# A gated GLU behind an FFT filter: x and the filter loaded as plain fp32 on one ordered SP queue, casts on GpSimd, and a main loop issued in the order it is written

## The chip, the core and the metric

The kernel runs on one NeuronCore of one Trainium2 chip. The metric is the device time of one execution in microseconds; before the change the median of 3 runs is 386.45 us (383.33 to 387.43).

## The reference

For `x` of shape (8, 3200, 256) in fp32, each channel is filtered along the sequence by a spectrum, and a causal gated linear unit follows:

```python
X = np.fft.rfft(x, axis=1)
y = np.fft.irfft(X * (filt_r + 1j * filt_i)[None], n=3200, axis=1)
gate_pre[s] = sum_k conv_w[k] * y_padded[s + k]          # 5 taps, causal
out = (sigmoid(gate_pre) * (y @ w_val)) @ w_out
```

## The kernel before

The transform of length 3200 is done as 128 x 25: a 128-point stage, a pass through a scratch in DRAM that reorders, and a 25-point stage; then the same backwards. Each batch goes through seven stages, and each stage cuts a batch into seven chunks, so that there are 56 chunks in all:

- `load_x` brings a chunk of `x` into a bf16 tile `xt` (4 or 3 rows of 256 for each of 128 partitions). It is issued on the GpSimd queue, whose DMA casts fp32 to bf16 on the way (line 86).
- `s1` multiplies `xt` by the constant `cf_t` (line 307), VectorE evicts PSUM into `so` (line 310), and SP writes `so` to the scratch `dscr` (line 312).
- `load_t` reads `dscr` back in another order into `tt` (lines 326 to 329). Each chunk of `tt` holds rows of all seven `dscr` writes of its batch.
- `s2` multiplies `tt` by `wc_t`, `ws_t`, `wsn_t` (lines 340 to 346). ScalarE evicts into `xs` (line 349). VectorE multiplies by the filter with two products `za`, `zb` and their sum `z` (lines 354, 358, 360). All three have two bf16 inputs in SBUF.
- `inva` is the inverse of that stage (lines 376, 378); ScalarE evicts into `u` (line 381), SP writes `escr` (line 392) and `load_v` reads it back into `vt` (line 398).
- `invb` is the inverse 128-point stage (line 413); ScalarE evicts into `yt` (line 415). For the first chunk of a batch GpSimd fills the four rows ahead of the sequence (a memset on line 420, two copies on line 422).
- `conv` (line 431, sigmoid on ScalarE on line 436), `val` (line 448, the product `gv` on VectorE on line 453) and `outp` (line 465) end the chunk; `o` is evicted by VectorE for even chunks (line 470) and by ScalarE for odd ones (line 473), and SP stores it (line 475).

Every matmul stage takes one tile `ps` from a PSUM pool of four tiles of 128 x 1024 fp32. A stage therefore may start only when the tile taken four stages earlier has been evicted.

A loop over G writes one chunk of each stage per step, with lags: `s1` works on chunk G, `s2` on G-9, `inva` on G-10, `invb` on G-19, `conv` on G-21, `val` on G-22, `outp` on G-23. Within a step the order is invb, s2, conv, s1, inva, val, outp. A scheduler then orders each engine's instructions by priority and by its own estimate of when they are ready; TensorE's and ScalarE's stand as written, but on VectorE `so` stands ahead of `z` in three of the seven steps of a batch. The seven `load_t` of a batch are issued together, and so are the seven `load_v`.

Ahead of the loop VectorE and ScalarE compute the transform matrices from iotas (`cf_t`, `wc_t` and so on). `floormod` (lines 103 to 113) takes seven VectorE instructions for each of six arguments; `expand` (line 171) makes a matrix with 13 instructions; `dg_t` (line 284) takes 20; `fm_t` (lines 232, 234) two large ones. The filter comes in 24 DMAs on the GpSimd queue, cast to bf16.

Of the kernel before, what the change touches and what calls it, by code (L numbers as in the profile page):

```python
# [15 lines left out]
PI = math.pi  # L16
# [19 lines left out]
def kernel(  # L36
# [31 lines left out]
    b_npi = cpool.tile([128, 1], FP32, name="b_npi")  # L68
# [3 lines left out]
    xpool = ctx.enter_context(tc.tile_pool(name="xin", bufs=10))  # L72
    spool = ctx.enter_context(tc.tile_pool(name="s1o", bufs=4))
    tpool = ctx.enter_context(tc.tile_pool(name="s2i", bufs=8))

    def psum():
        return pp.tile([128, 1024], FP32, name="ps", tag="ps")

# [3 lines left out]
    def load_x(b, j):  # L82
        p0, np_ = PCH[j]
        xt = xpool.tile([128, 4, D], BF16, name="xt")
        src = x[b].rearrange("(a r) d -> a r d", r=R)[:, p0:p0 + np_, :]
        nc.gpsimd.dma_start(out=xt[:, 0:np_, :], in_=src)  # L86
        xts[(b, j)] = xt

    for j in range(NCH):
        load_x(0, j)  # L90


    with tc.tile_pool(name="gen", bufs=1) as g1, \
         tc.tile_pool(name="gen2", bufs=2) as g2, \
         tc.tile_pool(name="genf", bufs=1) as gf:

        def floormod(src_ap, divisor):
            shp = list(src_ap.shape)
            divi = g2.tile(shp, I32, name=f"fm_i{shp[1]}")
            bak = g2.tile(shp, FP32, name=f"fm_b{shp[1]}")  # L100
            q = g2.tile(shp, FP32, name=f"fm_q{shp[1]}")
            cm = g2.tile(shp, FP32, name=f"fm_c{shp[1]}")
            nc.vector.tensor_scalar(divi[...], src_ap, 1.0 / float(divisor), None,
                                    op0=ALU.mult)
            nc.vector.tensor_copy(bak[...], divi[...])
            nc.vector.scalar_tensor_tensor(q[...], bak[...], -float(divisor), src_ap,
                                           op0=ALU.mult, op1=ALU.add)
            nc.vector.tensor_scalar(cm[...], q[...], float(divisor) - 0.5, None,
                                    op0=ALU.is_ge)
            nc.vector.scalar_tensor_tensor(q[...], cm[...], -float(divisor), q[...],  # L110
                                           op0=ALU.mult, op1=ALU.add)
            nc.vector.tensor_scalar(cm[...], q[...], -0.5, None, op0=ALU.is_lt)
            nc.vector.scalar_tensor_tensor(q[...], cm[...], float(divisor), q[...],
                                           op0=ALU.mult, op1=ALU.add)
            return q

        def iota(shape, pattern, base, cm, name):
            t = g1.tile(shape, FP32, name=name)
            nc.gpsimd.iota(t[...], pattern=pattern, base=base, channel_multiplier=cm,
                           allow_small_or_imprecise_dtypes=True)  # L120
            return t

        nc.vector.memset(b_npi[:, :], -PI)
        pcol = iota([128, 1], [[0, 1]], 0, 1, "pcol")


        kc = iota([128, NG, 2, GL], [[5, NG], [0, 2], [1, GL]], 1, 0, "kc")
        nc.vector.memset(kc[:, NG - 1, 0, GL - 1:GL], 0.0)
        pr = g1.tile([128, NG, 2, GL], FP32, name="pr")
        nc.vector.tensor_scalar(pr[...], kc[...], pcol[:, 0:1], None, op0=ALU.mult)  # L130
        nc.vector.tensor_scalar(pr[:, :, 0, :], pr[:, :, 0, :], 0.75 * L, None,
                                op0=ALU.add)
        q = floormod(pr[...].rearrange("p g c l -> p (g c l)"), L)
        nc.scalar.activation(cf_t[:, :], q[...], AF.Sin, bias=b_npi[:, 0:1],
                             scale=2.0 * PI / L)

        ident = g1.tile([128, 128], FP32, name="ident")
        nc.vector.memset(ident[:, :], 1.0)
        nc.gpsimd.affine_select(out=ident[:, :], in_=ident[:, :], pattern=[[1, 128]],
                                compare_op=ALU.is_equal, fill=0.0, base=0,  # L140
                                channel_multiplier=-1)
        idh = g1.tile([128, 128], FP16, name="idh")
        nc.vector.tensor_copy(idh[:, :], ident[:, :])


        rq = floormod(pcol[...], R)
        lp = g1.tile([128, 1], FP32, name="lp")
        nc.vector.tensor_tensor(lp[...], pcol[...], rq[...], op=ALU.subtract)
        nc.vector.tensor_scalar(lp[...], lp[...], 1.0 / R, None, op0=ALU.mult)
        rp = g1.tile([128, 1], FP32, name="rp")  # L150
        nc.vector.tensor_copy(rp[...], rq[...])
        lw = g1.tile([128, 1], FP32, name="lw")
        nc.vector.tensor_scalar(lw[...], pcol[...], 4.0 * R - 0.5, None, op0=ALU.is_ge)
        nc.vector.tensor_scalar(lw[...], lw[...], -65.0, None, op0=ALU.mult)


        mk = g1.tile([128, GL, R], FP16, name="mk")
        mkf = g1.tile([128, GL, R], FP32, name="mkf")
        nc.vector.memset(mkf[...], 1.0)
        nc.gpsimd.affine_select(out=mkf[...], in_=mkf[...], pattern=[[-R, GL], [0, R]],  # L160
                                compare_op=ALU.is_ge, fill=0.0, base=0,
                                channel_multiplier=1)
        nc.gpsimd.affine_select(out=mkf[...], in_=mkf[...], pattern=[[R, GL], [0, R]],
                                compare_op=ALU.is_ge, fill=0.0, base=R - 1,
                                channel_multiplier=-1)
        nc.vector.tensor_copy(mk[...], mkf[...])

        def expand(dst, src):
            nc.gpsimd.memset(dst[:, :, P2:128], 0.0)
            for g in range(NG):  # L170
                nc.vector.tensor_tensor(
                    dst[:, g, 0:P2].rearrange("p (l r) -> p l r", l=GL),
                    src[:, g, :].unsqueeze(1).to_broadcast((128, GL, R)),
                    mk[...], op=ALU.mult)

        def negate(dst, src):
            nc.vector.tensor_scalar(dst[...], src[...], -1.0, None, op0=ALU.mult)

        def sincos(prod, dc, ds, dsn):
            qs = floormod(prod[...].rearrange("p g r -> p (g r)"), N)  # L180
            sn = g2.tile([128, NG, R], FP16, name="sn")
            nc.scalar.activation(sn[...].rearrange("p g r -> p (g r)"), qs[...],
                                 AF.Sin, bias=b_npi[:, 0:1], scale=2.0 * PI / N)
            pc = g2.tile([128, NG, R], FP32, name="pc")
            nc.vector.tensor_scalar(pc[...], prod[...], 0.75 * N, None, op0=ALU.add)
            qc = floormod(pc[...].rearrange("p g r -> p (g r)"), N)
            cs = g2.tile([128, NG, R], FP16, name="cs")
            nc.scalar.activation(cs[...].rearrange("p g r -> p (g r)"), qc[...],
                                 AF.Sin, bias=b_npi[:, 0:1], scale=2.0 * PI / N)
            expand(dc, cs)  # L190
            expand(dsn, sn)
            negate(ds, dsn)

        HK = R // 2 + 1
        kv = g1.tile([128, NG, R], FP32, name="kv")
        nc.gpsimd.iota(kv[:, :, 0:HK], pattern=[[5, NG], [L, HK]], base=1,
                       channel_multiplier=0, allow_small_or_imprecise_dtypes=True)
        nc.gpsimd.iota(kv[:, :, HK:R], pattern=[[5, NG], [-L, R - HK]],
                       base=1 + L * (R - 1), channel_multiplier=0,
                       allow_small_or_imprecise_dtypes=True)  # L200
        nc.vector.tensor_scalar(kv[...], kv[...], lp[:, 0:1], None, op0=ALU.add)
        nc.vector.tensor_scalar(kv[:, NG - 1, :], kv[:, NG - 1, :], lw[:, 0:1], None,
                                op0=ALU.add)
        nc.vector.tensor_scalar(kv[...], kv[...], rp[:, 0:1], None, op0=ALU.mult)
        sincos(kv, wc_t, ws_t, wsn_t)


        fi_t = gf.tile([128, NG, D], BF16, name="fi_t")

        def fsrc(f, row, ap):  # L210
            return bass.AP(tensor=f.tensor, offset=f.offset + row * D, ap=ap + [[1, D]])

        for f, dst in ((filt_r, fr_t), (filt_i, fi_t)):
            for l in range(GL):
                ng = NG if l < GL - 1 else NG - 1
# [187 lines left out]
    def invb(b, j):  # L403
# [15 lines left out]
        if j == 0:  # L419
            nc.gpsimd.memset(y[:, :, 0:H, 0:1], 0.0)  # L420
            for dh in range(2):
                nc.gpsimd.tensor_copy(y[:, dh, 0:H, 1:L], y[:, dh, R:R + H, 0:L - 1])
# [68 lines left out]
    for G in range(total):  # L491
        c = at(G, -NCH)
        if c is not None:
            load_x(*c)
# [57 lines left out]
```

## Time and profile before

| | |
|---|---|
| median of 3 runs | 386.45 us |
| the profiled execution's own time | 387.95 us |
| its span, first to last instruction | 385.9 us |
| mean granted TensorE clock | 0.966 |
| busy: TensorE / VectorE / ScalarE / GpSimd | 312.3 / 284.9 / 229.1 / 64.2 us |
| first `s2` matmul | 45.09 us |
| first `invb` matmul | 92.66 us |
| GpSimd DMA issues of `xt` | 56, 30.2 us in all |
| GpSimd copies on line 422 | 16, 9.3 us in all |

The span is 2.05 us shorter than the profiled execution's time; that part lies outside the first and last instruction. Busy time of TensorE comes from modelled ends of pipelined matmuls, so a full digit in its row doesn't say that it runs at its peak. Idle time of an engine is put down to what released it last.

### The profile page before, as it was taken

The numbers are of one execution on the slowest core, as the hardware profiler recorded it, in microseconds if no ns is written. First come the engines' busy times: TensorE is split into PE (matmuls) and PEld (weight loads), VectorE is DVE, ScalarE is ACT, GpSimd is POOL, SyncE is SP. The second block draws the span as 40 slices with busy tenths as digits, with TensorE's granted clock in tenths as the row PEclk, the third lists the DMA queues.
The fourth block names the chain that finished last, engine by engine and source line by source line (L and its number), as shares of the span: only waits on it lengthen the run. The fifth ranks groups of instructions, "written<-read, shape, count | busy, mean of one in ns | idle before, by whom it ended". The sixth has DMA issues, their size and how long they took to land.

```text
span 385.9 us, 8019 instructions
## 1 busy us (share of the span) xinstructions
PE 312.3 (81%) x3089; PEld 206.9 (54%) x3089; DVE 284.9 (74%) x462; ACT 229.1 (59%) x255; POOL 64.2 (17%) x131
## 2 busy tenths in 40 slices
PE   0230477475899999999997999899999999999992
PEld 0100145253656756766675666566676677666661
DVE  4999958553858887888787789678977677765554
ACT  1100235334976777677765776677677878867660
POOL 8797211112110211021102011100010001001000
PEclk9999998766989999999999999999999999999998
DMA  7999999999999999999999999989595968449343
GB/s 124 144 162 190 216 257 251 231 250 280 179 250 249 311 286 273 263 282 332 274 301 303 286 269 298 285 299 319 201 351 170 304 223 299 136 142 323 141 191 152
DMA packets 94118, 94.53 MB, mean 245 GB/s; under 512 B 10102, under 2 KB 74624, under 8 KB 94080
## 3 DMA queue, kind: packets, MB, share of 16 engines
q1 hardware_dynamic: 80064, 78.98, 62.5%
q0 software_dynamic: 14016, 15.04, 28.1%
q8 instruction: 24, 0.39, 0.4%
q14 instruction: 14, 0.11, 0.1%
HBM read 56.59 MB, written 52.43 MB: 282 GB/s over the span
## 4 chain that ended last, share of the span: by engine, by line
PE 44%; DVE 20%; DMA 19%; SPq 8%; issue 4%; ACT 2%; POOL 1%; DVEq 0%; ACTq 0%; POOLq 0%
PE ps L431 12%; PE ps L448 7%; DMA escr<-u 6%; PE ps L465 6%; DVE so L310 6%; DMA vt<-escr 5%; SPq L326 5%; PE ps L413 5%; DMA dscr<-so 4%; PE ps L376 3%; DVE gv L453 3%; DMA tt<-dscr 3%; PE ps L378 3%; PE ps L307 3%; DVE za L354 2%
## 5 line engine op out<-in xcount | busy, mean ns | idle before, releaser
L415 ACT ACTIVATE yt<-ps 128x1024 bf16<-128x1024 f32 (+1 forms) x56 | 52.1, 931 | 44.3 <-PE ps L413 44.2
L453 DVE TENSOR_TENSOR gv<-ps,gt 128x1024 bf16<-128x1024 f32 (+1 forms) x56 | 61.9, 1104 | 18.7 <-PE ps L448 13.7
L310 DVE CAST so<-ps 128x1024 bf16<-128x1024 f32 (+1 forms) x56 | 61.5, 1103 | 19.0 <-PE ps L307 15.9
L354 DVE TENSOR_TENSOR za<-xs,fr_t 125x1024 bf16<-125x1024 bf16 (+1 forms) x56 | 37.3, 665 | 50.5 <-ACT xs L349 50.3
L381 ACT ACTIVATE u<-ps 125x1024 bf16<-125x1024 f32 (+1 forms) x56 | 53.9, 963 | 24.4 <-PE ps L378 21.6
L431 PE MATMUL ps<-yt,dg_t 64*64 64x512 bf16 (+1 forms) x1120 | 65.7, 361 | 0.8
L349 ACT ACTIVATE xs<-ps 125x1024 bf16<-125x1024 f32 (+1 forms) x56 | 54.0, 965 | 19.6 <-PE ps L346 18.4
L436 ACT ACTIVATE gt<-ps 128x1024 bf16<-128x1024 f32 (+1 forms) x56 | 52.4, 935 | 9.1 <-PE ps L431 5.9
L86 POOL DMA_DIRECT2D xt<-in_x_dram x56 | 30.2, 569 | 153.0 <-PE ps L307 146.5
L307 PE MATMUL ps<-xt,cf_t 128*128 128x512 bf16 x112 | 36.9, 421 | 22.4 <-DVE so L310 11.4
L465 PE MATMUL ps<-wo_t,gv 128*128 128x256 bf16 x400 | 52.8, 273 | 0.9 <-DVE gv L453 0.9
L448 PE MATMUL ps<-yt,wv_t 128*128 128x512 bf16 (+1 forms) x224 | 52.6, 357 | 0.0
L465 PEld LDWEIGHTS <-gv 128*128 128x128 bf16 x400 | 39.1, 98 | 14.9 <-DVE gv L453 1.2
L413 PE MATMUL ps<-ci_t,vt 128*128 128x128 f16 x400 | 31.9, 221 | 13.3 <-DMA vt<-escr 9.6
L431 PEld LDWEIGHTS <-dg_t 64*64 64x64 bf16 x1120 | 30.1, 106 | 23.2 <-issue 10.1
L340 PE MATMUL ps<-tt,wc_t 125*128 125x256 bf16 x104 | 30.1, 289 | 12.9 <-DMA tt<-dscr 10.6
L470 DVE COPY o<-ps 128x1024 f32<-128x1024 f32 (+1 forms) x32 | 36.7, 1148 | 1.1 <-PE ps L465 1.1
L360 DVE TENSOR_TENSOR z<-za,zb 125x1024 bf16<-125x1024 bf16 (+1 forms) x56 | 36.4, 650 | 1.3
L413 PEld LDWEIGHTS <-vt 128*128 128x128 bf16 x400 | 27.0, 98 | 17.9 <-DMA vt<-escr 10.7
L358 DVE TENSOR_TENSOR zb<-xs,fm_t 125x1024 bf16<-125x1024 bf16 (+1 forms) x56 | 36.2, 646 | 0.0
L376 PE MATMUL ps<-z,vc_t 125*128 125x256 bf16 x104 | 30.0, 289 | 6.9 <-DVE z L360 6.9
L307 PEld LDWEIGHTS <-cf_t 128*128 128x128 f16 x112 | 9.2, 108 | 41.7 <-issue 28.2
(109 smaller groups left out, 386.6 us busy)
## 6 DMA issues: line engine op xcount, KB each, us to landing
out_dram<-o SPq DMA_DIRECT2D x32, 512.0 KB
tt<-dscr SPq DMA_DIRECT2D x48, 256.0 KB
escr<-u SPq DMA_DIRECT2D x48, 224.0 KB
out_dram<-o SPq DMA_DIRECT2D x24, 384.0 KB
xt<-in_x_dram POOLq DMA_DIRECT2D x32, 256.0 KB, 6.5
dscr<-so SPq DMA_DIRECT2D x32, 256.0 KB
vt<-escr SPq DMA_DIRECT2D x32, 256.0 KB
xt<-in_x_dram POOLq DMA_DIRECT2D x24, 192.0 KB, 5.7
```

The source lines that it names most:

```text
L307: nc.tensor.matmul(ps[:, a * D:e * D], lhsT=cf_t[:, 0:128], rhs=xt[:, a:e, :], start=True, stop=True)
L310: nc.vector.tensor_copy(so[:, 0:np_, :].rearrange("p a d -> p (a d)"), ps[:, 0:np_ * D])
L349: nc.scalar.activation(xs[0:P2, 0:ng, :, :].rearrange("p g c d -> p (g c d)"), ps[0:P2, 0:ng * 512], AF.Copy)
L354: nc.vector.tensor_tensor(za[0:P2, 0:ng], xs[0:P2, 0:ng], fr_t[0:P2, g0:g0 + ng, :].unsqueeze(2).to_broadcast((P2, ng, 2, D)), op=ALU.mult)
L381: nc.scalar.activation(u[0:P2, 0:2 * ng, :].rearrange("p q d -> p (q d)"), ps[0:P2, 0:ng * 512], AF.Copy)
L413: nc.tensor.matmul(ps[:, o:o + L], lhsT=v[:, a, 128 * dh:128 * dh + 128], rhs=ci_t[:, :], start=True, stop=True)
L415: nc.scalar.activation(y[:, :, H + p0:H + p0 + np_, :].rearrange("p h a n -> p h (a n)"), ps[:, :].rearrange("p (h n) -> p h n", h=2)[:, : ...
L431: nc.tensor.matmul(ps[64 * dh:64 * dh + 64, 512 * r:512 * r + np_ * L], lhsT=dg_t[rows, dh, k, :], rhs=y[rows, dh, p0 + k:p0 + k + np_, :] ...
L436: nc.scalar.activation(g[:, :, 0:np_ * L], ps[:, :].rearrange("p (h n) -> p h n", h=2)[:, :, 0:np_ * L], AF.Sigmoid)
L448: nc.tensor.matmul(ps[:, 512 * eh:512 * eh + np_ * L], lhsT=wv_t[:, dh, 128 * eh:128 * eh + 128], rhs=y[:, dh, H + p0:H + p0 + np_, :], st ...
L453: nc.vector.tensor_tensor(gv[:, :, 0:np_ * L], ps[:, :].rearrange("p (h n) -> p h n", h=2)[:, :, 0:np_ * L], g[:, :, 0:np_ * L], op=ALU.mult)
L465: nc.tensor.matmul(ps[:, D * a:D * a + D], lhsT=gv[:, eh, L * a:L * a + L], rhs=wo_t[:, eh, :], start=(eh == 0), stop=(eh == 1))
```

## The change

- `load_x` is issued on SP, without a cast, into fp32 tiles `xf` (six buffers). A new stage `cast_x` on GpSimd copies `xf` into the bf16 `xt`, which has four buffers where it had ten.
- The filter is loaded as fp32 into `ff` by the same 24 transfers, on SP. VectorE casts the real part to `fr_t`, ScalarE makes `fm_t` from the imaginary part.
- `s1` of the first batch stands ahead of the computation of the other matrices; three of its seven evictions go to ScalarE. `load_t` of the first batch alternates with `load_x` of the second.
- The matrices are computed with three VectorE instructions in `sine` in place of seven in `floormod`, with one instruction per `expand` in place of 13, and with the negation and `dg_t` on ScalarE.
- The rows ahead of the sequence are filled by VectorE, in one memset and one copy.
- SP is issued in written order throughout, and in the main loop TensorE, ScalarE and VectorE too. Lags grow: `s2` 10, `inva` 11, `invb` 21, `conv` 23, `val` 24, `outp` 25. `load_t` and `load_v` are issued one chunk per step. `za` and `zb` have two buffers, `o` three.

```diff
@@ loads
-        xt = xpool.tile([128, 4, D], BF16, name="xt")
-        src = x[b].rearrange("(a r) d -> a r d", r=R)[:, p0:p0 + np_, :]
-        nc.gpsimd.dma_start(out=xt[:, 0:np_, :], in_=src)
-        xts[(b, j)] = xt
+        xf = fpool.tile([128, 4, D], FP32, name="xf")
+        src = x[b].rearrange("(a r) d -> a r d", r=R)[:, p0:p0 + np_, :]
+        nc.sync.dma_start(out=xf[:, 0:np_, :], in_=src)
+        xts[(b, j)] = xf
+
+    def cast_x(b, j):
+        np_ = PCH[j][1]
+        xf = xts[(b, j)]
+        xt = xpool.tile([128, 4, D], BF16, name="xt")
+        nc.gpsimd.tensor_copy(xt[:, 0:np_, :], xf[:, 0:np_, :])
+        xts[(b, j)] = xt
@@ s1
-        nc.vector.tensor_copy(so[:, 0:np_, :].rearrange("p a d -> p (a d)"),
-                              ps[:, 0:np_ * D])
+        if b == 0 and j % 2 == 1:
+            st[("Sact", j)] = nc.scalar.activation(sov, ps[:, 0:np_ * D], AF.Copy)
+        else:
+            nc.vector.tensor_copy(sov, ps[:, 0:np_ * D])
@@ ahead of the loop
+        for j in range(NCH):
+            s1(0, j)
+            if 1 <= j <= GL:
+                load_f(j - 1)
...
+        for j in range(NCH):
+            load_t(0, j)
+            load_x(1, j)
@@ invb
-            nc.gpsimd.memset(y[:, :, 0:H, 0:1], 0.0)
-            for dh in range(2):
-                nc.gpsimd.tensor_copy(y[:, dh, 0:H, 1:L], y[:, dh, R:R + H, 0:L - 1])
+            nc.vector.memset(y[:, :, 0:H, 0:1], 0.0)
+            nc.vector.tensor_copy(y[:, :, 0:H, 1:L], y[:, :, R:R + H, 0:L - 1])
@@ main loop
+    steps = [
+        (invb, LAG_IB, 0), (s2, LAG_S2, 0), (conv, LAG_IB + 2, 0), (cast_x, -2, 1),
+        (s1, 0, 1), (inva, LAG_S2 + 1, 0), (load_x, -NCH, 2), (load_t, NCH, 1),
+        (load_v, LAG_S2 + 1 + NCH, 0), (val, LAG_IB + 3, 0), (outp, LAG_IB + 4, 0),
+    ]
+    with tc.manual_schedule(engines={E.SP, E.PE, E.Activation, E.DVE}):
+        for G in range(total):
+            for stage, lag, first in steps:
+                c = at(G, lag, first)
+                if c is not None:
+                    stage(*c)
```

## The prediction

> **What bounds the kernel now.** I read the slices of the page first, then the chain of work that ended last, then the timeline around single steps.
>
> ```profile
> PE   0230477475899999999997999899999999999992
> DVE  4999958553858887888787789678977677765554
> DMA  7999999999999999999999999989595968449343
> ```
>
> A slice is 9.65 us. TensorE hardly works for four slices and is half used up to the tenth: that is the filling of the pipeline. From about 100 us on it shows nines. The DMA engines look full for most of the span, but the digit is the time that packets were under way. What the queues moved for it:
>
> ```profile
> q1 hardware_dynamic: 80064, 78.98, 62.5%
> q0 software_dynamic: 14016, 15.04, 28.1%
> ```
>
> q1 is SP's: 62.5% of 385.9 us is 241 us for 78.98 MB, 3.05 us per MB. q0 is GpSimd's casting queue: 108 us for 15.04 MB as written, 7.2 us per MB. The chain tells which of the full-looking resources sets the pace:
>
> ```profile
> 88.33 4.28 DMA vt<-escr
> 92.66 1.03 PE ps L413 x8
> ...
> 176.43 1.23 DVE so L310
> 178.34 0.89 ACT yt L415
> 179.28 1.03 ACT xs L349
> 180.33 0.69 DVE za L354
> 182.27 1.22 DVE so L310
> ```
>
> Up to 92.66 us the first batch runs through two DRAM scratches; then `invb` starts, and 293.2 us remain. Within these the same ring comes back in each step: `so` frees the PSUM tile that the next `invb` takes (four tiles later), `invb` and `s2` run on TensorE, `yt` and `xs` on ScalarE, then `za`, `zb`, `z` and again `so` on VectorE. From one `so` to the next: 1.23 (`so`) + 0.68 (`invb`, with its hand-over) + 0.94 (`yt`) + 1.05 (`xs`) + 1.94 (from `za` to the next `so`) = 5.84 us. The batch's `vt` reads stand in the chain at 163.22, 203.33 and 242.89: 40 us per batch, 5.7 per step. So neither the matmul sum nor the DMA sum binds there, but this ring, and whatever lengthens `za`, `zb`, `z` on VectorE lengthens the step.
>
> One thing already does so now:
>
> ```profile
> 180.33 0.69 DVE L354 TENSOR_TENSOR za<-xs,fr_t 125x1024 bf16<-125x1024 bf16 x1 [0.96 <-ACT xs L349]
> ...
> 231.98 0.60 PE L307 MATMUL ps<-xt,cf_t 128*128 128x512 bf16 x2
> 232.00 0.69 DVE L354 TENSOR_TENSOR za<-xs,fr_t 125x1024 bf16<-125x1024 bf16 x1 [0.84 <-ACT xs L349]
> 232.88 0.53 POOL L86 DMA_DIRECT2D xt<-in_x_dram  x1 [5.03 <-PE ps L307]
> ...
> 248.93 1.16 POOL L422 COPY yt<-yt 128x508 bf16<-128x508 bf16 x2 [10.32 <-ACT yt L415]
> 249.81 0.82 DVE L354 TENSOR_TENSOR za<-xs,fr_t 125x1024 bf16<-125x1024 bf16 x1 [1.95 <-ACT xs L349]
> ```
>
> `za` takes 0.69 us, but 0.82 where GpSimd's copies on line 422 are still running. They end at 250.09; `za` ends at 250.63, 0.54 us later, and 0.54 is what 1024 elements take without the 0.15 of start. In the other batches (`za` at 169.42 and so on) it ends 0.54 to 0.55 us after the copy too. So a two-input VectorE instruction stands still until a GpSimd copy is through.
>
> **The change part by part.** Times are span times; the profiled run is 387.95 with a span of 385.9, the median of the runs 386.45, and I add the difference to the median.
>
> *Filling, up to the first `s2`.* Before, the first `tt` is issued at 34.18 and `s2` starts at 45.09. After, GpSimd stands in this order: four casts, then the iotas and selects that the matrices need. `x` lands from about 4 us, the casts end near 8.5, five small ones (0.35 each) near 10.5, so VectorE's first `so` comes near 12. Then VectorE has, ahead of the seventh `so`: four `expand` (13 x 0.14 us = 1.82 before, about 1.75 each in one instruction, 7.0), four `sine` groups (0.24 + 0.24 + 0.24 + 0.41 each, 4.5), three `so` (3.4), odds and ends and waits for ScalarE's sines (3): 18 us, to 30. That `so` takes 1.2 and its `dscr` lands 3.1 later (the chain's row): `tt` is issued near 34.5, no earlier than now. What left VectorE (`floormod`'s four extra instructions, `dg_t` 4.0, `fm_t` 3.9) is paid for by having all matrices ahead of that `so`. ScalarE's additions (20 `dg_t`, two negations, `fm_t`, three `so`, about 18 us by 0.83 us per 1000 elements from its 1.02 us rows) lie in the 31 us that it idles between 12 and 45 us. In the written order three `s1` of batch 1 stand ahead of the first `s2`; the third waits for three `tt` and three `x` on the one queue, 3 x (0.243 + 0.468) MB x 3.05 = 6.5 us, a receipt and a cast: `s2` near 45. Gain 0, bounds -4 and +4.
>
> *Filling, from `s2` to `invb`.* Now 45.1 to 92.7, 47.6 us. After, 11 steps without `conv`, `val`, `outp`; per step SP's queue carries `x` 0.468, `dscr` 0.234, `tt` 0.243, `escr` 0.229 MB = 1.17 MB x 3.05 = 3.6 us, more than any engine has. 11 x 3.6 + 2 for the last read = 41: `invb` at 86.2, a gain of 6.5. GpSimd's casts (next part) raise VectorE's share of a step from 3.2 to 4.1, and it takes over the pace for some of them: +3.
>
> *The DMA side in the loop.* `x` costs 13.1 MB x 7.2 = 94 us of the engines now, and 26.2 x 3.05 = 80 after. SP's issues grow by 80; at 0.3 to 0.5 us each a full step has seven, 3 us of 5.8. In SP's order `load_t` waits for the last `dscr`, and `dscr`, `escr`, `x`, `vt` and `out` stand behind it; the write was issued a step earlier and takes 3 to 5 us, and `tt` has three steps (17 us) until `s2`. Cost 0; without that lead some 4 us per batch. [...]
>
> *Written order.* Only VectorE's order changes: `z` always ahead of `so`, where three steps of a batch have `so` first. That is 0 to 3 x 0.69 us per batch; these three are the narrow steps (`so` 0.95 in place of 1.22), which leave room, so I take 0.7, 3.5 over five batches. The longer lags make two steps fewer in which all stages run together, each lighter by about 1.0 us: -2. VectorE's copy of the edge rows (0.6 to 1.1 us, by `z` and `so` rows of its size) falls in its wait for `xs` (50.3 us in 39 times), and the 0.13 us of blocking by line 422 goes: -0.5. Together +1, bounds -6 and +8.
>
> *The casts.* No row shows one. GpSimd's copy of 508 elements takes 0.61, a memset of 8 takes 0.14: 0.945 us per 1000 and 0.13 of start, so 1.10 us for 1024 and 0.86 for 768. The other end is its select on fp32, 128 elements in 0.35, 1.7 us per 1000: 1.87 us. I take the copy, the same operation. When does it run? `xt` has four buffers, so the cast of chunk G+4 is released by `s1` of chunk G, as line 86 is now: 0.90 us after the start of that matmul (231.98, 232.88). `za` starts about with that matmul (232.00), `zb` 0.61 later. So the cast is asked for while `zb` runs, takes its place when `zb` ends and before `z`, which waits for `zb`, can start, and `z` stands still until it is through. The loss is the cast less the 0.15 us of start that `z` has behind it: 0.95 in the four wide steps, 0.71 in the three narrow, 5.9 us per batch. The step with the half `s2` chunk hides its 0.95, and I take off 0.5 for room in the narrow ones: 4.4. Casts run four chunks ahead and end at step 51; from step 21 that is 31 steps, 4.4 batches: **+19.4 us**. Bounds: 0, if the cast waits until `z` is done and runs beside `so`, which reads PSUM; 5.9 x 4.4 = 26; with the slow cast (1.72 and 1.28 lost per step, 10.7 per batch) 47.
>
> [...] The rows above show only the case where GpSimd was first. [...]
>
> Sum: 0 - 6.5 + 3 + 1 + 19.4 = **+17 us**: span 403, median 386.45 + 17 = **403 us**.
>
> **The rivals.**
>
> *The casts fit into gaps (faster).* GpSimd gets the port only when `z` is done, or the casts drift to where VectorE reads PSUM (`so`, `gv`, `o`, about 3.4 us of a wide step). For it: 1.0 us of cast has room in a step of 5.8. Against it: VectorE idles just before `z`, waiting for `zb`, and that is when the cast is waiting. The place is the ring of each step; it decides as soon as less than 5.5 / 4.4 = 1.25 us per batch is lost. Then 0 - 6.5 + 1 = -5.5: 381 us.
>
> *The cast is slow.* At 1.7 us per 1000 elements the loss is near 35 in the loop and 8 in the filling: -6.5 + 8 + 1 + 35 = 37, about 424 us. Against it, that row is a select, not a copy.
>
> *One queue blocks itself.* Each of seven batches loses 4 us while SP waits for `dscr` or `escr` to land: 28 us without any blocking by casts, 409 us. The lead of three steps speaks against it.
>
> **How the numbers follow.** Forecast 0.57, casts in gaps 0.32, slow cast 0.08, blocked queue 0.03. The forecast's own range is 393 to 416. The gap case spreads over 375 to 388 by the bounds of the filling and the order. From 376 to 418 lie nearly all of the forecast, three quarters of the gap case and the queue case: 8 in 10. A difference of 1% (382.6 and 390.3) is about what a measurement tells here. Faster: 0.26, all from the gap case; within 1%: 0.07, its upper end and the forecast's lowest; slower: 0.67.
>
> **What would show it.** In the profile after, the timeline should show `z` or `zb` on VectorE at 1.3 to 1.7 us beside a GpSimd copy of 1.1, in most steps; the tile `z` should have a median far over 0.69. `so` to `so` should be 6.6 in wide steps, a batch 44 to 45 us. The first `invb` should start between 84 and 93 us. If `zb` and `z` stay at 0.69 and a batch at 40, the step on the casts is wrong and the time is near 381. If the first `s2` comes well before 41 us, the step on the filling is wrong. If TensorE's waits for `tt` or `vt` grow, it is the queue.

## The result and the profile after

| | before | after |
|---|---|---|
| median, 4 runs each on one chip | 385.11 us (383.33 to 387.43) | 408.05 us (407.39 to 408.72) |
| ratio, 95% interval | | 1.059 (1.052 to 1.066) |
| span of the profiled execution | 385.9 us | 405.7 us |
| first `s2` matmul | 45.1 us | 57.9 us |
| from there to the first `invb` | 47.6 us | 45.5 us |
| from the first `invb` to the end | 293.2 us | 302.3 us |

The change makes the kernel 22.9 us slower; the two profiled spans differ by 19.8 us. The forecast was 403 us, with +17. The total came out near that, and two terms of the sum did not: the start lost 12.8 us where the forecast had 0, and the rest lost less than it had. (Below, medians are of all executions and ratios leave out those over 1.5% longer than the fastest of their kernel; the profiles of `e8_both_lags` and `e12_filter_split` are of such slower ones, so their stage times are rough.)

The slices of the page again, 10.14 us each (TensorE, VectorE, DMA):

```profile
PE   3200056746599888898898899897999999999993
DVE  2970139958759887988988978987898687754554
DMA  8798699897999999999999999999778978758544
```

TensorE has three slices of nothing, from 20 to 51 us, and VectorE a 0 and a 1 in the last two of them. Before, VectorE was full until 48 us. The cheaper matrices were ready early (the last one at 27.2 us), and nothing could use them. The queues:

```profile
q1 hardware_dynamic: 91678, 108.52, 85.5%
q0 software_dynamic: 1408, 0.26, 1.0%
```

`x` and the filter have gone from GpSimd's queue to SP's, 108.52 MB in place of 78.98. The chain of work that ended last names what filled the empty slices, and then a piece of the steady loop:

```profile
17.02 7.98 DMA dscr<-so
25.02 10.13 DMA ff<-in_filt_i_dram
35.17 7.88 DMA ff<-in_filt_r_dram
...
43.12 3.61 DMA dscr<-so
...
46.78 0.39 SPq L148
...
216.46 0.69 DVE za L378
217.15 1.45 DVE zb L382
218.66 0.57 issue
219.24 0.96 DVE so L133
```

The last `dscr` write of batch 0 is issued at 43.12 us, behind all 24 transfers of the filter, and the first `tt` at 46.78; before, `tt` was issued at 34.18. In the loop it is the same ring as before, with a `zb` of 1.45 us in it, counted from the end of `za`, where it was 0.6 before. The timeline of that step:

```profile
216.46 0.69 DVE L378 TENSOR_TENSOR za<-xs,fr_t 125x1024 bf16<-125x1024 bf16 x1 [0.32 <-ACT xs L373]
...
216.80 1.25 POOL L98 CAST xt<-xf 128x1024 bf16<-128x1024 f32 x1 [4.33 <-PE ps L126]
...
217.07 1.53 DVE L382 TENSOR_TENSOR zb<-xs,fm_t 125x1024 bf16<-125x1024 bf16 x1
...
218.63 0.69 DVE L384 TENSOR_TENSOR z<-za,zb 125x1024 bf16<-125x1024 bf16 x1
...
219.24 0.95 DVE L133 CAST so<-ps 128x768 bf16<-128x768 f32 x1
```

GpSimd's cast is asked for at 216.80 while `za` runs. It takes 1.25 us where an undisturbed one takes 1.04: it waits for `za`. Then `zb` stands still until the cast is through (218.05) and ends 0.55 us later, the 0.54 that the prediction read from its rows. So each holds up the other, and the order of arrival decides. The groups (busy us, mean ns):

```profile
L98 POOL CAST xt<-xf 128x1024 bf16<-128x1024 f32 (+1 forms) x56 | 60.6, 1084 | 214.8 <-PE ps L126 147.2
...
L384 DVE TENSOR_TENSOR z<-za,zb 125x1024 bf16<-125x1024 bf16 (+1 forms) x56 | 49.6, 885 | 1.9
...
L382 DVE TENSOR_TENSOR zb<-xs,fm_t 125x1024 bf16<-125x1024 bf16 (+1 forms) x56 | 46.0, 821 | 0.0
```

Before, `z` took 36.4 us in all and `zb` 36.2. A mean hides the pattern, since 33 of the 112 are over 0.75 us and the others are unchanged. In `s2` of batches 2 to 5 (counted from 0, steps too) each of the 28 steps has one: `z` in steps 0, 1, 5 and 6 and `zb` in steps 2, 3 and 4, but for step 0 of batch 2, where it is `zb`. Together that is 4.9 us a batch. The batch period there is 42.6 us. The other five lie in batch 0, during the filling, where seven `za` of batches 0 and 1 are longer too (0.78 to 1.20 us).

### The profile page after: what moved, and what is told of

It is laid out like the page before. It is cut to its first block, busy times and chain, and to the rows that moved or that the text cites. A ratio compares the mean times of both kernels' runs of the same rounds, so it can differ in the third digit from the quotient of the medians.

```text
span 405.7 us, 8039 instructions
## 1 busy us (share of the span) xinstructions
PE 308.1 (76%) x3089; PEld 202.7 (50%) x3089; DVE 296.0 (73%) x381; ACT 247.1 (61%) x282; POOL 70.0 (17%) x83
## 3 DMA queue, kind: packets, MB, share of 16 engines
q1 hardware_dynamic: 91678, 108.52, 85.5%
## 4 chain that ended last, share of the span: by engine, by line
PE 36%; DVE 24%; DMA 21%; issue 7%; ACT 6%; SPq 4%; POOL 1%; DVEq 0%; ACTq 0%
DVE so L133 10%; PE ps L454 9%; PE ps L471 6%; PE ps L488 5%; DVE zb L382 5%; PE ps L437 5%; DMA dscr<-so 5%; ACT xs L373 4%; DVE za L378 4%; DMA vt<-escr 4%; DMA tt<-dscr 4%; DMA xf<-in_x_dram 3%; DMA ff<-in_filt_i_dram 2%; PE ps L364 2%; DMA ff<-in_filt_r_dram 2%
## 5 line engine op out<-in xcount | busy, mean ns | idle before, releaser
L98 POOL CAST xt<-xf 128x1024 bf16<-128x1024 f32 (+1 forms) x56 | 60.6, 1084 | 214.8 <-PE ps L126 147.2
L126 PE MATMUL ps<-xt,cf_t 128*128 128x512 bf16 x112 | 35.6, 405 | 48.4 <-POOL xt L98 46.9
L133 DVE CAST so<-ps 128x1024 bf16<-128x1024 f32 (+1 forms) x53 | 58.5, 1104 | 9.4 <-DMA tt<-dscr 6.8
L384 DVE TENSOR_TENSOR z<-za,zb 125x1024 bf16<-125x1024 bf16 (+1 forms) x56 | 49.6, 885 | 1.9
L382 DVE TENSOR_TENSOR zb<-xs,fm_t 125x1024 bf16<-125x1024 bf16 (+1 forms) x56 | 46.0, 821 | 0.0
L454 PEld LDWEIGHTS <-dg_t 64*64 64x64 bf16 x1120 | 29.0, 107 | 24.3 <-issue 10.9
L400 PE MATMUL ps<-z,vc_t 125*128 125x256 bf16 x104 | 28.7, 276 | 6.9 <-DVE z L384 6.0
```

What stands on the lines that cost most here:

```text
L98: nc.gpsimd.tensor_copy(xt[:, 0:np_, :], xf[:, 0:np_, :])
L133: nc.vector.tensor_copy(sov, ps[:, 0:np_ * D])
L382: nc.vector.tensor_tensor(zb[0:P2, 0:ng], xs[0:P2, 0:ng, ::-1, :], fm_t[0:P2, g0:g0 + ng], op=ALU.mult)
L454: nc.tensor.matmul(ps[64 * dh:64 * dh + 64, 512 * r:512 * r + np_ * L], lhsT=dg_t[rows, dh, k, :], rhs=y[rows, dh, p0 + k:p0 + k + np_, :] ...
```

## The experiments

Two theories. *A*: GpSimd's copies hold up `zb` and `z`, and this is what the loop loses. *B*: the filter's transfers on SP stand ahead of `dscr`, and this is what the start loses. Against A: the written order, the lags or the single queue cost the loop. Against B: the moved `s1`, the matrices, or `x` of batch 1 make the first `s2` late. Ratios are to the kernel before, run on the same chip.

**x back on the casting queue, and no copies (`e1_x_cast_dma`).**

```diff
-        nc.sync.dma_start(out=xf[:, 0:np_, :], in_=src)
+        nc.gpsimd.dma_start(out=xt[:, 0:np_, :], in_=src)      # ten xt buffers
-        (cast_x, -2, 1),
```

> The changed kernel with x loaded by GpSimd's casting DMA straight into ten bf16 buffers, as before the change; no cast copies at all. Theory A (the copies hold VectorE's zb and z up, 23.6 us of VectorE time, and that is the loop's loss): zb and z fall back to 0.69 us in all steps, the stretch from the first invb to the end goes from 302 to about 293 us, the first s2 stays at 58: about 399 us. Rival A' (the written order, the longer lags or the one SP queue cost the loop, and the blocking is covered by slack): the stretch stays near 302, about 407 us.

Measured 397.22 us, ratio 1.031 (1.024 to 1.038). No `zb` or `z` is over 0.75 us; from the first `invb` (105.0) to the end 290.8 us in place of 302.3; the first `s2` is still late, at 59.9. In the loop it is as A says.

**The filter back on the casting queue (`e2_filter_cast_dma`).**

```diff
-                nc.sync.dma_start(out=dst[...], in_=fsrc(...))   # fp32, all 24
+                nc.gpsimd.dma_start(out=dst[...], in_=fsrc(...)) # into fr_t and fi_t, bf16
```

> The changed kernel with the filter's 24 transfers issued on GpSimd's casting queue as before the change, and x still on SP. Theory B (the filter's transfers stand on SP ahead of the last dscr writes and hold up the first tt): the last dscr is issued near 30 us, the first s2 starts near 45 in place of 58, about 396 us; the stretch from the first invb stays at 302. Rival B' (the first s2 is late because of the matrices, the first batch's s1 moved ahead of them, or x of batch 1 between the tt loads): the first s2 stays near 57, about 408 us.

Measured 407.1 us, ratio 1.057 (1.053 to 1.062): nothing gained, though the first `s2` comes at 51.0. From this alone B would have fallen. Its trace shows another wait in place of the one removed: 24 issues of 0.6 us now stand on GpSimd ahead of the selects of the matrices and of batch 1's copies. These copies then run in one go, beside the matrices (timeline):

```profile
40.13 6.45 DVE L248 TENSOR_TENSOR wc_t<-cs,mk 128x1625 f16<-128x1625 f16 x1
...
40.97 1.11 POOL L98 CAST xt<-xf 128x1024 bf16<-128x1024 f32 x1
...
42.09 6.14 POOL L98 CAST xt<-xf 128x1024 bf16<-128x1024 f32 x6
...
46.50 2.63 DVE L248 TENSOR_TENSOR ws_t<-sn,mk 128x1625 f16<-128x1625 f16 x1
```

An instruction of 1.03 us (its time in the changed kernel) lasts 6.45: five copies run one after another in that time, and it ends while the sixth, which takes 1.66 us, is under way. So the one that waits doesn't get its turn after each copy.

**Both back (`e3_both_cast_dma`).**

> Both of the former at once: x and the filter on GpSimd's casting queue; what is left of the change is the written order, the lags, the cheaper matrices and s1 of the first batch ahead of them. Theories A and B: first s2 near 45, the stretch from the first invb near 293, about 386 us, no different from the kernel before. If the written order itself costs or saves, it shows here alone: by A' and B' about 407 us.

Measured 381.87 us (10 runs), ratio 0.992 (0.987 to 0.997): a little faster than before. First `s2` 38.5, first `invb` 88.4, 290.1 us from there. What is left of the change (written order, lags, matrices and the moved `s1`) costs nothing.

**The copies kept, but beside `so` (`e4_cast_after_z`).** The copy of each step waits for that step's `z`, so it meets an instruction that reads PSUM.

```diff
+        c = nc.gpsimd.tensor_copy(xt[:, 0:np_, :], xf[:, 0:np_, :])
+        tc.add_manual_dep(c.ins, st["zins"].name, ...)           # z of this step
```

> The changed kernel with all its copies on GpSimd, but each copy in the main loop waits for z of the same step, so that it runs beside so, which reads PSUM. Theory A: zb and z fall to 0.69 us although every copy is still there, the stretch from the first invb goes from 302 to 293 to 296 us, the first s2 stays at 58: 399 to 402 us. Rival A': the stretch stays near 302, 408 us. Rival A'' (the copy is asked for too late and s1 waits for xt): over 410 us, with TensorE waiting for GpSimd.

Measured 398.33 us, ratio 1.038 (1.033 to 1.042); from the first `invb` 292.6 us. The timeline (`cast_x` is line 95 here):

```profile
216.63 0.68 DVE L382 TENSOR_TENSOR zb<-xs,fm_t 125x1024 bf16<-125x1024 bf16 x1
...
217.35 0.69 DVE L384 TENSOR_TENSOR z<-za,zb 125x1024 bf16<-125x1024 bf16 x1
...
217.96 1.22 DVE L133 CAST so<-ps 128x1024 bf16<-128x1024 f32 x1
...
218.26 1.03 POOL L95 CAST xt<-xf 128x1024 bf16<-128x1024 f32 x1 [4.55 <-DVE z L384]
```

All 56 copies are there, `so` keeps its 1.22 us beside them, and `zb` and `z` keep theirs. With the run without copies this shows that it is when the copies run that costs the loop, not that they run.

**A copy, and a memset, added to the kernel without copies (`e6_extra_copy`, `e7_extra_memset`).**

```diff
+        c = nc.gpsimd.tensor_copy(dm[:, 0:np_, :], dsrc[:, 0:np_, :])   # e6; e7: nc.gpsimd.memset(dm[:, 0:np_, :], 0.0)
+        tc.add_manual_dep(c.ins, mm.ins.name, ...)                      # last s1 matmul
```

> The kernel with x and the filter on the casting queue (381.9 us, first invb at 88.4, 290 us from there), plus one copy per main-loop step on GpSimd from a constant fp32 tile to an unused bf16 tile, released by the step's last s1 matmul, until s1 ends; nothing reads it. Theory A (the copy alone makes zb and z wait, whatever brought x): zb or z over 0.75 us in half of the steps, the stretch from the first invb 299 to 302, about 391 to 394 us. Rival (the loss came of the copies together with fp32 x on SP, or with s1 waiting for them): the stretch stays at 290 to 291, 382 to 383 us.

> As the kernel before it, but the extra GpSimd instruction is a memset of 1024 or 768 fp32 elements to an unused tile: it writes SBUF and reads nothing, released in the same place. If what VectorE's two-input instructions and GpSimd share is the reading side: zb and z stay at 0.69 us, 382 to 383 us. If any GpSimd instruction on SBUF holds them up: as with the copy, in proportion to its duration.

Measured 401.88 us for the copy, ratio 1.042 (1.035 to 1.049), and 382.47 for the memset, 0.991 (0.986 to 0.995). One step of each (copy, then memset; the lines stand 9 further down):

```profile
214.32 0.69 DVE L387 TENSOR_TENSOR za<-xs,fr_t 125x1024 bf16<-125x1024 bf16 x1 [1.45 <-ACT xs L382]
...
214.77 1.14 POOL L133 CAST dm<-dsrc 128x1024 bf16<-128x1024 f32 x1 [4.70 <-PE ps L129]
...
214.93 1.52 DVE L391 TENSOR_TENSOR zb<-xs,fm_t 125x1024 bf16<-125x1024 bf16 x1
```

and with the memset:

```profile
209.00 0.69 DVE L387 TENSOR_TENSOR za<-xs,fr_t 125x1024 bf16<-125x1024 bf16 x1
...
209.45 0.95 POOL L133 MEMSET dm<- 128x1024 f32 x1 [4.04 <-PE ps L463]
...
209.61 0.69 DVE L391 TENSOR_TENSOR zb<-xs,fm_t 125x1024 bf16<-125x1024 bf16 x1
...
210.33 0.69 DVE L393 TENSOR_TENSOR z<-za,zb 125x1024 bf16<-125x1024 bf16 x1
```

The same place and nearly the same length; what reads SBUF doubles `zb` (1.52 us), what only writes leaves it alone (0.69; no `zb` or `z` of that run is over 0.75). So the copy costs by itself, whatever brought `x`, and between these two instructions it is the reading that makes the difference. The copy cost more than expected (20 us against 9 to 12): the batch period is 42.6 us, the same as in the changed kernel, but it holds for one batch more (four full periods, three there), and 5.7 us are lost ahead of the first `invb` (94.1 against 88.4).

**The filter's bytes spread differently on SP (`e5_filter_125`, then `e9_filter_112`).** The same 3.3 MB in 1024-byte pieces in the same places on SP, but not to 13 or 12 partitions a transfer. In both runs the rows come to lie in other partitions than the products need, so the output isn't the filtered one; everything behind the load does the same work. The first try went to 125:

```diff
-                    out=dst[R * l:R * l + HK, 0:ng, :], in_=...      # 13 or 12 partitions
+                    out=ff[0:P2, c, a:e, :], in_=...                 # e5: 125 partitions
+                    out=ff[0:112, c, a:e, :], in_=...                # e9: 112, the last 13 in two more
```

> The changed kernel, but the filter's bytes come in 10 transfers to 125 partitions each, in place of 24 to 13 or 12; still on SP, in the same places, still 3.3 MB in 1024-byte pieces. The filter rows are permuted by this. Theory B1 (the narrow destination makes a 1024-byte packet take 104 ns, and this paces SP at 1.2 us an issue): packets take some 50 ns, the last dscr of batch 0 is issued near 31 us in place of 43, the first s2 starts near 46 to 48, the first invb near 92 to 94, about 397 us. Theory B2 (it is the bytes of the filter, or the number of pieces, whatever their destination): packets stay near 100 ns, the first s2 stays at 55 to 58, 405 to 408 us.

Measured 413.41 us, ratio 1.072 (1.064 to 1.081): worse, first `s2` 61.6. Both theories named in that expectation missed. Packets did fall, from 98 ns in the mean (median 94) to 48 (median 46); the expectations say 104 and 49. But the packet records show that between 28 and 48 us 5.0 of them run at a time on average (in the changed kernel 10.3 between 14 and 43 us, most often 13). SP's issues got longer:

```profile
22.31 4.63 SPq L134 DMA_DIRECT2D dscr<-so  x1
26.98 0.33 SPq L189 DMA_DIRECT2D ff<-in_filt_r_dram  x1
27.35 4.10 SPq L189 DMA_DIRECT2D ff<-in_filt_i_dram  x1
```

13 and 5 divide the numbers of partitions, 13 and 125. The next try took 112, where the kernel itself splits its `escr` writes (line 412 of the changed kernel); that 16 packets would run at a time there was the author's expectation, and no run shows it (10.1, below).

> As the run with 125 partitions, where exactly 5 packets ran at a time at 49 ns each (against 13 at 104 ns in the changed kernel), but the same bytes go to 112 partitions, and in two further transfers to the other 13. The filter rows are permuted by this. Theory B1' (what paces SP is how many DMA engines a transfer is spread over: 13 for 13 partitions, 5 for 125): 16 packets run at a time at 50 to 60 ns, the last dscr of batch 0 is issued at 29 to 33 us in place of 43, the first s2 starts at 45 to 49, the first invb at 90 to 95, 394 to 399 us. Rival B2 (the bytes or the number of pieces on the one queue set the pace): last dscr near 43, first s2 near 58, 408 us.

Measured 397.2 us, ratio 1.031 (1.023 to 1.039). SP's queue in the timeline of the changed kernel:

```profile
22.32 0.31 SPq L190 DMA_DIRECT2D ff<-in_filt_r_dram  x1
23.61 0.30 SPq L193 DMA_DIRECT2D ff<-in_filt_r_dram  x1
25.02 0.31 SPq L190 DMA_DIRECT2D ff<-in_filt_i_dram  x1
26.95 0.30 SPq L193 DMA_DIRECT2D ff<-in_filt_i_dram  x1
28.47 0.35 SPq L134 DMA_DIRECT2D dscr<-so  x1
...
43.12 0.35 SPq L134 DMA_DIRECT2D dscr<-so  x1
46.78 0.39 SPq L148 DMA_DIRECT2D tt<-dscr  x1
```

and with 112 partitions:

```profile
25.25 0.34 SPq L134 DMA_DIRECT2D dscr<-so  x1
26.27 0.33 SPq L189 DMA_DIRECT2D ff<-in_filt_r_dram  x1
26.83 0.31 SPq L189 DMA_DIRECT2D ff<-in_filt_i_dram  x1
28.42 0.34 SPq L134 DMA_DIRECT2D dscr<-so  x1
33.27 0.39 SPq L148 DMA_DIRECT2D tt<-dscr  x1
```

An issue takes 0.3 us in both, but in the changed kernel the next mostly comes only 0.9 to 1.9 us later: SP waits without the profile naming a releaser. With 112 partitions the gaps are nearly as long at the end (0.6 to 1.7 us), but each issue brings more bytes: 12 transfers in place of 24. The last `dscr` goes out at 28.42 and the first `s2` starts at 45.07, the time that the prediction had. So it is neither the bytes nor the move to SP as such that costs the 12.8 us: it is the pace of the filter's narrow transfers on a queue on which `dscr` stands behind them.

What made the pace better isn't the number of engines that B1' names: 10.1 packets run at a time on average between 14 and 33 us, as many as in the changed kernel, but one takes 59 ns in the mean in place of 98. The two runs also have fewer transfers and read neighbouring rows of DRAM, where in the changed kernel the rows of one partition and the next lie 128 rows apart. Fewer transfers alone don't help (the 10 of the run with 125 were the slowest). Against the distance of the rows stands that the run with 112 still has two transfers to 13 partitions, issued at 14.61 and 15.64 us, from neighbouring rows too: 196 of its 3250 packets take over 105 ns, 136 of them within 17.4 to 19 us, where the run with 125, which has no such transfer, has 1 (7 in all). The records don't name a packet's transfer, so this speaks for the few partitions and doesn't prove them.

**Both causes taken out of the changed kernel (`e11_beside_so_filter_later`).** Copies beside `so`, and the filter on the casting queue behind the matrices' small GpSimd work.

```diff
-            if 1 <= j <= GL:
-                load_f(j - 1)
...
         vs_ins = sincos(nc.vector, nv, vc_t, vs_t, vsn_t)
+        for l in range(GL):
+            load_f(l)                                    # on GpSimd, casting
```

> The changed kernel with the copies waiting for z (398.3 us, first s2 58, first invb 102.8, 292.6 from there), and the filter's transfers on GpSimd's casting queue behind the matrices; x stays on SP in fp32. By theories A and B together: no filter on SP, so first s2 at 45 to 49, first invb at 90 to 95, the rest 293: 385 to 390 us, that is the time before the change. If batch 1's copies, which now stand behind 32 DMA issues on GpSimd, are what is late: first s2 at 50 to 54, 392 to 396 us.

Measured 384.61 us, ratio 1.000 (0.995 to 1.004); first `s2` 44.3, first `invb` 88.2, 295.3 us from there. With the two causes gone the changed kernel stands where the kernel before does, with `x` in fp32 on SP and all copies still in it. Here the last `dscr` goes out by 21.5 and the first `tt` at 26.64; what then holds the first `s2` is the copies of batch 1, which begin at 40.32, behind GpSimd's issues.

**Shorter lags, and two tries at a better start (`e8_both_lags`, `e10_both_filter_later`, `e12_filter_split`),** all from the 381.87 us kernel.

> The kernel with x and the filter on the casting queue (381.9 us), with the lags of the kernel before the change (s2 9, inva 10, invb 19). Two steps fewer in all, and one s1 of batch 1 fewer ahead of the first s2. If a step of the filling is worth 3 to 5 us, first invb near 80 to 83 and 374 to 378 us; if the filling is bound by the arrival of batch 1's x and of tt, or if one step of lead too few makes s2 wait for tt in the loop, 381 to 386 us.

Measured 421.08 us, ratio 1.083 (1.070 to 1.097). The first `invb` did come earlier (86.7), and then TensorE waits for `vt` (its waits, in us, times, longest):

```profile
PE ps L437 <- DMA vt<-escr: 46.3, 23, 6.9
```

It was 6.3 us in 5 times with the longer lags. All lags go back together, so `load_t` loses a step of lead too, but TensorE's waits for `tt` hardly grow (9.6 us to 11.8). With SP's queue in written order, a lead of two steps in place of three between a `load_v` and its `invb` costs the loop some 35 to 40 us.

> The kernel with x and the filter on the casting queue (381.9 us, first s2 38.5, first za 46.7, first invb 88.4), with the filter's transfers emitted behind the matrices, so that GpSimd makes the selects, iotas and memsets of the matrices and four x of batch 1 first. If in that kernel the matrices' wait for GpSimd behind 24 issues held up the start: matrices done near 35 us in place of 46, first za near 40 to 43, first invb 82 to 86, 376 to 380 us. If the arrival of the filter holds it instead, it now arrives later: first za 45 to 48, 381 to 384 us.

Measured 383.37 us, ratio 0.995 (0.991 to 1.000). The matrices were ready, the first `s2` came at 35.6, and the filter was what was late:

```profile
34.49 7.15 DMA fi_t<-in_filt_i_dram
...
41.75 3.07 ACT fm_t L335
44.81 2.97 ACT fm_t L337
...
47.81 0.70 DVE zb L384
```

> The kernel with x and the filter on the casting queue (381.9 us, first s2 38.5, first za 46.7, first invb 88.4), with the filter divided: the imaginary part stays on GpSimd's casting queue, the real part comes in fp32 on SP between the dscr writes, 12 transfers in place of the 24 that cost 12.8 us there. If the two queues share the work: GpSimd is through with the filter some 8 us earlier, SP is held up by 5 to 6 us, first za at 42 to 45, first invb 84 to 87, 377 to 380 us. If half of the transfers on SP hold the dscr writes up as long as the gain on GpSimd is: first s2 at 44 to 48, 382 to 386 us.

Measured 385.26 us, ratio 1.002 (0.998 to 1.006); the first `s2` moved back to 49.4. Twelve narrow transfers on SP cost somewhat more than they relieve GpSimd of (the median is 3.4 us higher). By its median the kernel with both loads back on the casting queue remains the best; the one with the later filter can't be told from it.

## Why the prediction was right in sum, and where its steps failed

The difference of the two spans by stage, predicted and measured. The last two rows divide 302.3 - 293.2 = +9.1 with the 290.1 of the kernel with both loads back:

| step | predicted | measured |
|---|---|---|
| up to the first `s2` | 0 (-4 to +4) | +12.8 |
| from `s2` to `invb` | -6.5 + 3 = -3.5 | -2.1 |
| written order and lags | +1 (-6 to +8) | -3.1 |
| casts in the loop | +19.4 (0 to 26, or 47) | +12.2 |
| sum | +17 | +19.8 |

- *Up to the first `s2`*: **the step that failed.** It followed VectorE to the seventh `so` and took `tt` as issued when that lands. VectorE was even earlier: 1.02 to 1.04 us for an `expand`, predicted 1.75. What was left out are the 24 filter transfers on the same queue, ahead of that last `dscr`: the step priced neither their issues nor their bytes. With the same bytes in wide transfers (`e9`) its numbers come out: `tt` at 33.27 (predicted 34.5), `s2` at 45.07 (predicted 45). From the filter's first issue to the last `dscr` the changed kernel took 29 us for these 3.3 MB (14.05 to 43.12), `e9` 14.3 (14.10 to 28.42). The prediction also named only an early first `s2` as the sign of an error; it came late.
- *From `s2` to `invb`*: right in sign, 1.4 us short.
- *The DMA side in the loop*: cost 0 held within the 3 us of the next point, and its reason, the lead of three steps, is borne out: with two (`e8`, there with `x` on the casting queue) the loop lost 35 to 40 us, more than the 28 of the rival of a blocked queue.
- *Written order*: inside its bounds. The -3.1 rests on single profiles; the profiles of other kernels without the blocking gave 289 to 295 us from the first `invb`, so this row and the next are known to some 3 us. By the medians, all that is left of the change without its two loads is worth -2.9 us (381.87 against 384.76).
- *Casts*: that they hold up `zb` and `z` is shown (`e1`, `e4`, `e6`, `e7`), **the size was off**. That a cast asked for during a VectorE instruction takes its place when that one ends, on which the 19.4 rests, was the author's estimate, and no row of the kernel before shows it; in the changed kernel the cast at 216.80 took 1.25 us in place of 1.04, through the end of `za`, and the `zb` behind it 1.53 in place of 0.69. Of the port that the first rival names the runs show these waits and no more. The duration was right (1.04 and 0.83 us, predicted 1.10 and 0.86). The wait comes to 4.9 us a batch (predicted 5.9). The prediction had every cast arrive during `zb` and hold up `z`; in three of seven steps it arrived during `za` and held up `zb`, so the median of `z` stayed at 0.69, against the predicted sign. Of the 4.9, about 3 reach the period (42.6 us against 39.4, 39.9 and 38.5 in `e3`, and 39.4 to 40.0 in `e1`), predicted 4.4. In `e1` VectorE idles on average 7.8 us per batch (39.8 less 32.0 busy), in the changed kernel 5.9: the ring had 2 us of room, not 1.5. And the blocking held for four batches of `s2`, taken as 4.4; 4 x 3 = 12.
- *The signs*: `zb` or `z` at 1.3 to 1.7 us in most steps came out at 1.15 to 1.53 in 33 of 56; so-to-so of 6.6 us in wide steps at 5.4 to 6.6, 6.1 on average; a batch of 44 to 45 us at 42.6; and the first `invb`, expected by 93, at 103.4, because of the first step.

That the sum came within 5 us of the measured median is luck in part: an error of +12.8 in one term against two of -4.1 and -7.2 in others.

## What to carry to other kernels

When a load is moved to another queue, write down that queue's whole order with the number of partitions of each transfer beside it, and ask what stands behind the narrow ones; put a load with 13 or 125 partitions a transfer where nothing urgent follows it (the first `s2` came at 57.9 and 61.6 us behind such transfers, at 45.07 behind twelve of which ten went to 112). An engine that is mostly idle (GpSimd, 17% busy) isn't free: its copy (0.83 or 1.04 us) beside VectorE instructions with two SBUF inputs made one of them wait 0.5 to 0.84 us in each of the 28 steps above, of which some six tenths reached the loop, and the same copy placed beside a PSUM eviction (`so`, 1.22 us with it) cost nothing that can be measured here (292.6 us from the first `invb`, other kernels without the blocking 289 to 295). When a removed cost doesn't come back as time, as with the filter alone on GpSimd, look for the wait that took its place before dropping the theory.

## What was not expected of the hardware

- A 1024-byte packet of the filter took 98 ns in the mean in transfers to 13 or 12 partitions and 48 ns to 125, yet the second was slower in all, with 5 packets at a time. The median of the first, 94 ns, is above the 89 ns of the changed kernel's 2048-byte packets in the first 45 us. That the few partitions make it, and not the rows' distance in DRAM, is likely by the run with 112 but not shown.
- A VectorE instruction of 1.03 us stood for 6.45 us beside six GpSimd copies in a row and didn't get a turn after each, while a single copy in the changed kernel delayed one instruction once (`zb` 1.53 us in place of 0.69).
- A GpSimd memset of 0.95 us beside `zb` cost VectorE nothing (0.69 us), and a copy of 1.14 us made it 1.52.
